# Product groups of 384 tokens that begin after three of batch 0's five query blocks

## The chip, the cores and the metric

One core of one Trainium2 chip runs the whole program. The metric is the device time in microseconds of one execution. TensorE (PE) multiplies and transposes, VectorE (DVE), ScalarE (ACT) and GpSimd (POOL) work on tiles, SyncE (SP) issues DMAs. ACT and POOL issue some DMAs too.

## The reference

Attention with a forgetting gate over 8 batches, 8 heads, 576 tokens and head width 64, then a two-layer product with a SiLU over all 4608 tokens.

```python
scores = scale * np.matmul(q, k.transpose(0, 1, 3, 2))
cum = np.cumsum(np.log(np.clip(f, 0.0001, 1.0)), axis=-1)
scores = np.where(causal, -1000000000.0, scores + cum[:, :, :, None] - cum[:, :, None, :])
attn = softmax(scores)                      # over the last axis
x = (attn @ v).transpose(0, 2, 1, 3).reshape(4608, 512)
h = x @ w_in                                # w_in 512 x 2048
out = (h * sigmoid(h)) @ w_out              # w_out 2048 x 512, out float32
```

All inputs are float32. The gate factors into a row factor, which the softmax cancels, and a column factor exp(-cum), which the kernel multiplies into v.

## The kernel before

The work on attention goes by **pairs** p of heads: four pairs in a batch, 32 in all. 576 tokens are five blocks, four of 128 and one of 64 (the tail).

For the first batches q and k come as float32 by SP (`load_main` into `whole`, `load_tail` into one of two `raw` tiles), POOL casts them (`cast_main`, `cast_tail`), TensorE transposes them (`turn_first`, `transposes`, result `tpqk`), and DVE copies them to qT and kT. Later batches come by casting DMAs on POOL's queue (`load_qk`, tiles `mp`) and DMA transposes on SP.

The decay is made once for all batches: `decay_clip`, `decay_sum`, `decay_turn`, result wT, the exps in L180 and L183. `prep_v(p)` on POOL multiplies v (vm) with wT into one of the `vaug` tiles, with wT itself as a 65th column.

`scores(p, t)` makes the transposed scores of pair p in four tiles t (TensorE L281, one exp each on ACT, L306, result uT). `attend_rows` multiplies with vaug (L349, `avr`), and DVE divides by the 65th column (L358, L359, result `xt`). `turn_pair` turns the rows to xT (TensorE `tpx` L371, ACT copy L377).

The product goes by **groups** g of TG = 512 tokens. `m1_chunk(g, fc)` is one of 16 chunks of the first layer: four matmuls (`hp`, L400), tanh on ACT (L411), one DVE operation (L412, result `gtile`). `m2_part(g, tb, part)` is a quarter of the second layer for 128 tokens: four matmuls (`po`, L425) with four of the 16 rows of w_out. After four parts ACT scales the result and SP writes it.

The order is written by hand: the program text under `manual_schedule` is the order on each engine, and each engine runs its list in order. So is each queue of DMA issues, SP's and POOL's. A DMA that must wait for a free tile holds up all issues behind it.

In front, batch 0 runs whole: all four pairs, all five blocks, then `m1_chunk(0, 0)` begins. Between the parts of batch 1 and later `work(n)` puts n chunks or parts, from two lists `m1_queue` and `m2_queue`; a group's second layer may begin when its first is through (`can_m2`). `pace(p)` says how many a pair gets; m1_ready says how many groups have their xT. Batch 1 can draw on group 0 alone.

The loads of the weights are on POOL's queue: w_in in two halves after the casts of pair 2, ahead of `prep_v(0)`; w_out in four quarters by rows (`load_rows`) behind these lines:

```python
cast_both(NPB)
cast_both(NPB + 1)
prep_v(NPB)
for c in range(0, NFC, NFC // 4):
    load_rows(w_out_bf, moe_w_out, c, c + NFC // 4)
```

`prep_v(NPB)` is that of pair 4, batch 1's first, and reads v of batch 1. The SP queue has batch 1's loads in the order tails, q and k (`load_main`), v.

Of the kernel before, what the change touches and what calls it, by code (L numbers as in the profile page):

```python
# [15 lines left out]
P = 128  # L16
# [3 lines left out]
def kernel(  # L20
# [38 lines left out]
    NVA = 3  # L59
# [4 lines left out]
    xp = ctx.enter_context(tc.tile_pool(name="xp", bufs=4))  # L64
# [4 lines left out]
    evp = ctx.enter_context(tc.tile_pool(name="evp", bufs=2))  # L69
    rp = ctx.enter_context(tc.tile_pool(name="rp", bufs=4))  # L70
    gpool = ctx.enter_context(tc.tile_pool(name="gpool", bufs=2))
# [6 lines left out]
    MOST = 9.0  # L78
    HOLD = 6
# [43 lines left out]
    def load_qk(b, c, which):  # L123
        t = sbp.tile([P, DM], BF16, name="mp", tag="mp", bufs=16)
        raw[b, c, which] = t
        nc.gpsimd.dma_start(  # L126
            out=t[: bs[c], :].rearrange("p (h d) -> p h d", h=H),
            in_=(q, k)[which][b, :, c * P : c * P + bs[c], :].rearrange("h p d -> p h d"),
        )
# [9 lines left out]
    f_sb = evp.tile([BH, S], FP32, name="f_sb", tag="ev")  # L139
# [14 lines left out]
    def decay_sum():  # L154
        lnf = f_sb
        cum = evp.tile([BH, S], FP32, name="cum", tag="ev")
        nc.vector.tensor_tensor_scan(
            out=cum[:, :], data0=lnf[:, :], data1=lnf[:, :], initial=0.0,
            op0=ALU.add, op1=ALU.bypass,
        )  # L160
        mid = const.tile([BH, 1], FP32, name="mid")
        nc.vector.tensor_scalar_mul(out=mid[:, :], in0=cum[:, S - 1 : S], scalar1=0.5)
        cumc = cum
        nc.vector.tensor_scalar(
            out=cumc[:, :], in0=cum[:, :], scalar1=mid[:, 0:1], scalar2=None,
            op0=ALU.subtract,
        )
        cums.append(cumc)
# [20 lines left out]
    def cast_main(b, j, which):  # L189
        m = sbp.tile([P, NB * 2 * D], BF16, name="m", tag="m", bufs=4)  # L190
        m = m.rearrange("p (c h d) -> p c h d", c=NB, h=2)
        cast[b, j, which] = m
        nc.gpsimd.tensor_copy(  # L193
            out=m[:, 0 : NB - 1, :, :].rearrange("p c h d -> p h c d"),
            in_=whole[b][:, which, 2 * j : 2 * j + 2, :].rearrange(
                "p h (c d) -> p h c d", c=NB - 1
            ),
        )

    def cast_tail(b, j, which):  # L200
        m = cast[b, j, which]
        nc.gpsimd.tensor_copy(
            out=m[:TAIL, NB - 1, :, :], in_=tails[b, which][:TAIL, 2 * j : 2 * j + 2, :]
        )

    def turn_first(which):
        qk_tiles(0) if 0 not in qkT else None
        m = cast[0, 0, which].rearrange("p c h d -> p c (h d)")
        tp = big([P, SM], BF16, "tpqk")
        for c in range(NB - 1):  # L210
            nc.tensor.transpose(tp[:, c * P : (c + 1) * P], m[:, c, :], ident_bf[:, :])
        nc.vector.tensor_copy(
            out=qkT[0][which][:, 0, 0:SM].rearrange("x (p c) -> x p c", c=NB - 1),
            in_=tp[:, :].rearrange("x (c p) -> x p c", c=NB - 1),
        )

    def turn_first_tails():
        tp = big([P, 2, TAIL], BF16, "tpqk")
        for which in range(2):
            m = cast[0, 0, which].rearrange("p c h d -> p c (h d)")  # L220
            nc.tensor.transpose(
                tp[:, which, :], m[:TAIL, NB - 1, :], ident_bf[:TAIL, :TAIL]
            )
        for which in range(2):
            nc.vector.tensor_copy(out=qkT[0][which][:, 0, SM:S], in_=tp[:, which, :])

    def transposes(p, which):
# [5 lines left out]
        for c in range(NB):  # L233
            n = bs[c]
            nc.tensor.transpose(  # L235
                tp[:, c * P : c * P + n], m[:n, c, :, :].rearrange("p h d -> p (h d)"),
                ident_bf[:n, :n],
            )
        dst = qkT[b][which][:, j, :]
# [6 lines left out]
    def prep_v(p):  # L246
# [3 lines left out]
        for c0, c1, n in ((0, NB - 1, P), (NB - 1, NB, TAIL)):  # L250
# [8 lines left out]
        nc.gpsimd.tensor_copy(  # L259
            out=va[:, :, :, D], in_=wT[:, :, 2 * j + b * H : 2 * j + 2 + b * H]  # L260
# [9 lines left out]
    def scores(p, t):  # L270
        qT, kT = (x[:, p % NPB, :] for x in qkT[p // NPB])
        u = us[p % 3]
        first = p < NPB
        sc = psc.tile([P, 2, 512], FP32, name="sc", tag="sc")
        adds = ([(0, P)], [(64, P)], [(0, P), (320, P)], [(0, TAIL)])[t]
        pe_adds = adds if first and t == 2 else []
        col = 0
        for kb, q0, n in TILES[t]:
            for i in range(2):
# [6 lines left out]
                    stop=not pe_adds,  # L286
                )
            for i in range(2) if pe_adds else ():
                nc.tensor.matmul(  # L289
                    sc[:, i, col : col + P],  # L290
                    lhsT=ident_bf[:, :],
                    rhs=maskadd[:, :],
                    start=False,
# [4 lines left out]
        if first and not pe_adds:  # L298
            for c0, nk in adds:
                nc.vector.tensor_tensor(  # L300
                    out=sc[:nk, :, c0 : c0 + nk],
                    in0=sc[:nk, :, c0 : c0 + nk],
                    in1=maskadd[:nk, None, 0:nk].to_broadcast([nk, 2, nk]),
                    op=ALU.add,
                )
# [3 lines left out]
        if first:  # L309
            return  # L310
# [11 lines left out]
    TG = 512  # L322
# [14 lines left out]
    def attend_rows(p, lohi=((0, 3), (3, NB))):  # L337
        b, j = divmod(p, NPB)
        u, va = us[p % 3], vaugs[p % NVA]
# [26 lines left out]
    def turn_pair(p):  # L366
        b, j = divmod(p, NPB)
        tp = big([P, S], BF16, "tpx")
        for c in range(NB):
# [6 lines left out]
        for x, at, o, n in x_parts(b * S, (b + 1) * S):  # L376
# [64 lines left out]
    m2_queue = [(g, tb, pt) for g in range(NG) for tb in range(4) for pt in range(4)]  # L441
# [17 lines left out]
    def can_m1():  # L459
# [3 lines left out]
        return g < m1_ready and (not m2_queue or m2_queue[0][0] > max(g - 2, min(g - 1, 0)))  # L463
# [4 lines left out]
    def work(n):  # L468
        nonlocal turn_m2
        for _ in range(n):  # L470
            if can_m2() and (turn_m2 or not can_m1()):
                m2_part(*m2_queue.pop(0))
                turn_m2 = False
            elif can_m1():
                m1_chunk(*m1_queue.pop(0))
                turn_m2 = True
            else:
                return
            spend(0.88)

    def have():
        return sum(1 for x in m1_queue + m2_queue if x[0] < m1_ready)

    def pace(p):
# [7 lines left out]
        for _ in range(20):  # L492
            k = NPB * (b + 1) - p + min(LAG, 3.5 * (b - 1)) / (2.3 + 0.88 * n)
# [58 lines left out]
    with tc.manual_schedule():  # L552
        nc.scalar.dma_start(out=f_sb[:, :], in_=f.rearrange("b h s -> (b h) s"))
        load_main(0, 0, 2)
        load_tail(0)
        load_main(0, 2, 4)
        for c in range(2):
            load_v(0, c, nc.sync)
        load_main(0, 4, H)
        for c in range(2, NB):  # L560
            load_v(0, c, nc.sync)

        def cast_both(p):
# [3 lines left out]
            for w in RAW[b]:  # L567
                cast_tail(b, j, w)
# [6 lines left out]
        for u in us:  # L575
            nc.vector.memset(u[:, :, uoff[4] + TAIL :], 0.0)
        for va in vaugs:
# [8 lines left out]
        for w in range(2):  # L586
            cast_main(0, 0, w)
        for w in range(2):
            cast_tail(0, 0, w)
        cast_both(1)  # L590
        cast_both(2)
        load_w(w_in_bf, moe_w_in, 0, DFF // 2)
        load_w(w_in_bf, moe_w_in, DFF // 2, DFF)
        for w in range(2):
            turn_first(w)
        scores(0, 0)
        turn_first_tails()
        scores(0, 1)
        decay_sum()
        scores(0, 3)  # L600
        transposes(1, 0)
        scores(0, 2)
        decay_turn()
        prep_v(0)
        transposes(1, 1)
        scores(1, 0)
        cast_both(3)
        load_tail(1)
# [4 lines left out]
        for p in range(1, NPB):  # L613
            more = p + 1 < NPB
            prep_v(p)
            scores(p, 1)
            if more:
                transposes(p + 1, 0)
            scores(p, 3)
            if more:  # L620
                transposes(p + 1, 1)
            if p > 1:
                turn_pair(p - 2)
            attend_rows(p - 1, LO)
            scores(p, 2)
            if more:
                scores(p + 1, 0)
            attend_rows(p - 1, HI)
        turn_pair(NPB - 2)
        attend_rows(NPB - 1, LO)  # L630
        attend_rows(NPB - 1, HI)
        m1_chunk(0, 0, begin=True)
        turn_pair(NPB - 1)
        m1_ready = 1
        cast_both(NPB)
        cast_both(NPB + 1)
# [3 lines left out]
        work(HOLD)  # L640
        transposes(NPB, 0)
        work(1)
        transposes(NPB, 1)
        work(2)
        due = 0.0
        for p in range(NPB, NP):
# [4 lines left out]
            due += pace(p)  # L651
            n = int(due)
            due -= n
            n1, n2 = (n + 2) // 3, (n + 1) // 3
            n3 = n - n1 - n2
# [15 lines left out]
            if p == NPB * NEARLY - 3:  # L671
                load_tail(NEARLY)
                load_main(NEARLY, 0, 4)
                load_main(NEARLY, 4, H)
            for fn in fetch.get(p, []):
                fn()
            if early:
                work(n2 // 2)
# [7 lines left out]
            work(n2 - n2 // 2 if early else n2)  # L686
# [6 lines left out]
            if j == NPB - 1:  # L693
                attend_rows(p)
                spend(1.2)
                if b < NTURN:
                    work(2)
# [4 lines left out]
        while m1_queue or m2_queue or later:  # L702
            n = len(m1_queue) + len(m2_queue)
            work(1)
# [30 lines left out]
```

## Time and profile before

| what | us |
|---|---|
| median of 3 runs | 359.93 (359.5 to 360.38) |
| profiled execution, its own time | 359.25 |
| its span, first to last instruction | 357.5 |
| first dense product (hp) on PE | 34.12 |
| first po on PE | 53.8 |
| end of the last matmul | about 354 |
| w_in issued / w_out issued on POOL | 14.39 / 41.33 |

The page gives busy time by engine and the span in 40 slices of 8.94 us; a digit is the busy share in tenths. A timeline line has start, length, engine, line of the code, operation, out<-in, count, and in brackets the idle time before it with what ended it. "to landing" is the time from the issue of a DMA to its completion.

### The profile page before, as it was taken

To read this page: it belongs to the slowest core of one execution; us is meant where nothing else is said; L and a number is where in the kernel's file an instruction comes from. 1 tells how busy PE (TensorE), PEld (TensorE's weight loads), DVE (VectorE), ACT (ScalarE), POOL (GpSimd) and SP (SyncE) were. 2 spreads that over 40 slices of the span, in tenths; PEclk is the share of its full clock that TensorE was granted. 3 is DMA by queue.
4 is the path that set the end of the run, shared out by engine and by line. 5 is a ranking of instruction groups with operands and counts; after the bars stand their busy time and mean duration, and the time that the engine had idled before them with its cause. 6 is when DMAs were issued, how large, how long until landed. Compare 5 with 4: busy or idle time off the path is not lost.

```text
span 357.5 us, 7026 instructions
## 1 busy us (share of the span) xinstructions
PE 336.3 (94%) x2656; PEld 168.4 (47%) x2697; DVE 191.7 (54%) x450; ACT 211.9 (59%) x345; POOL 119.6 (33%) x207
## 2 busy tenths in 40 slices
PE   2797989999999999999999999999999999999995
PEld 1455445554555445544454453444444454444442
DVE  4664895538743675348543791567237723744300
ACT  4566674558753986388647764676468615644421
POOL 5563598239554235423564250110301000000000
PEclk9999999999999999999999999999999999999999
DMA  8899999999997998399969994452240014000021
GB/s 220 213 208 315 192 193 222 155 210 170 148 150 117 163 150 78 89 170 142 124 122 152 130 166 123 100 117 75 74 83 31 1 68 118 2 29 29 31 76 71
DMA packets 142514, 44.92 MB, mean 126 GB/s; under 512 B 129616, under 2 KB 136784, under 8 KB 142480
## 3 DMA queue, kind: packets, MB, share of 16 engines
q1 hardware_dynamic: 87664, 33.64, 42.5%
q0 software_dynamic: 54736, 10.69, 38.4%
q8 instruction: 21, 0.34, 0.4%
q10 hardware_dynamic: 80, 0.15, 0.2%
q14 instruction: 13, 0.11, 0.1%
HBM read 36.85 MB, written 9.44 MB: 129 GB/s over the span
## 4 chain that ended last, share of the span: by engine, by line
PE 82%; DVE 6%; ACT 4%; DMA 3%; issue 3%; POOL 1%; SPq 0%; ACTq 0%
PE po L425 33%; PE hp L400 30%; PE avr L349 7%; PE sc L281 7%; DVE gtile L412 2%; ACT uT L306 2%; DMA xT<-xt 2%; PE tpx L371 2%; DVE uT L320 2%; PE tpqk L235 2%; ACT th L411 1%; DMA whole<-in_k_dram 1%; DVE xt L359 1%; PE sc L289 1%; DVE qT L240 1%
## 5 line engine op out<-in xcount | busy, mean ns | idle before, releaser
L400 PE MATMUL hp<-xT,w_in_bf 128*128 128x512 bf16 x556 | 135.8, 380 | 3.2 <-DVE gtile L412 0.8
L425 PE MATMUL po<-w_out_bf,gtile 128*128 128x512 bf16 x555 | 133.7, 379 | 1.4 <-DVE gtile L412 0.4
L412 DVE SCALAR_TENSOR_TENSOR gtile<-th,hp 128x512 bf16<-128x512 bf16 x144 | 96.0, 685 | 52.2 <-ACT th L411 50.3
L306 ACT ACTIVATE uT<-sc 128x1024 bf16<-128x1024 f32 (+1 forms) x128 | 101.3, 850 | 24.9 <-PE sc L281 15.9
L411 ACT ACTIVATE th<-hp 128x512 bf16<-128x512 f32 x144 | 84.8, 613 | 50.0 <-PE hp L400 46.2
L251 POOL TENSOR_TENSOR vaug<-vm,wT 128x512 bf16<-128x512 f32 x64 | 45.4, 729 | 132.7 <-PE avr L349 121.4
L400 PEld LDWEIGHTS <-w_in_bf 128*128 128x128 bf16 x576 | 53.1, 98 | 65.2 <-issue 6.1
L425 PEld LDWEIGHTS <-gtile 128*128 128x128 bf16 x576 | 53.6, 98 | 62.9 <-issue 2.4
L320 DVE TENSOR_TENSOR uT<-uT,mask 128x256 bf16<-128x256 bf16 (+1 forms) x112 | 35.3, 337 | 66.2 <-ACT uT L306 66.0
L434 ACT ACTIVATE osb<-po 128x512 f32<-128x512 f32 x36 | 21.7, 602 | 46.7 <-PE po L425 46.7
L281 PE MATMUL sc<-qT,kT 64*128 64x64 bf16 (+4 forms) x384 | 37.3, 287 | 5.5 <-ACT uT L306 2.2
L349 PEld LDWEIGHTS <-uT 128*128 128x128 bf16 x960 | 33.7, 98 | 6.4 <-issue 0.7
L349 PE MATMUL avr<-vaug,uT 128*128 128x65 bf16 x960 | 36.2, 195 | 0.2 <-POOL vaug L259 0.2
L359 DVE TENSOR_TENSOR xt<-avr,rr 128x384 bf16<-128x384 f32 x64 | 31.4, 491 | 2.3
L281 PEld LDWEIGHTS <-kT 64*128 64x128 bf16 x384 | 15.3, 95 | 30.1 <-issue 21.0
L126 POOL DMA_DIRECT2D mp<-in_k_dram x30 | 25.9, 865 | 1.0 <-DMA mp<-in_k_dram 1.0
L126 POOL DMA_DIRECT2D mp<-in_q_dram x25 | 22.2, 887 | 1.3 <-DMA w_out_bf<-in_moe_w_out_dram 0.5
L358 DVE RECIPROCAL rr<-avr 128x6 f32<-128x6 f32 x64 | 11.7, 183 | 18.6 <-PE avr L349 18.5
L377 ACT COPY xT<-tpx 128x512 bf16<-128x512 bf16 (+7 forms) x32 | 11.2, 404 | 17.0 <-PE tpx L371 16.9
L193 POOL CAST m<-whole 128x512 bf16<-128x512 f32 x20 | 11.9, 607 | 15.0 <-DMA whole<-in_q_dram 12.4
L235 PE MATMUL tpqk<-ident_bf,m 128*128 128x128 bf16 (+1 forms) x90 | 10.9, 241 | 0.3 <-DVE gtile L412 0.3
L235 PEld LDWEIGHTS <-m 128*128 128x128 bf16 (+1 forms) x90 | 7.3, 106 | 6.3 <-issue 1.6
(47 smaller groups left out, 71.8 us busy)
## 6 DMA issues: line engine op xcount, KB each, us to landing
out_dram<-osb SPq DMA_DIRECT2D x36, 256.0 KB, 2.2
vm<-in_v_dram SPq DMA_DIRECT2D x32, 256.0 KB, 4.7
mp<-in_k_dram POOLq DMA_DIRECT2D x24, 128.0 KB, 6.2
whole<-in_q_dram SPq DMA_DIRECT2D x5, 512.0 KB, 9.7
mp<-in_q_dram POOLq DMA_DIRECT2D x20, 128.0 KB, 4.8
w_in_bf<-in_moe_w_in_dram POOLq DMA_DIRECT2D x2, 1024.0 KB, 11.2
w_out_bf<-in_moe_w_out_dram POOLq DMA_DIRECT2D x4, 512.0 KB, 10.7
whole<-in_k_dram SPq DMA_DIRECT2D x3, 512.0 KB, 9.5
```

What stands on the lines that cost most here:

```text
L126: nc.gpsimd.dma_start(out=t[: bs[c], :].rearrange("p (h d) -> p h d", h=H), in_=(q, k)[which][b, :, c * P : c * P + bs[c], :].rearrange("h ...
L235: nc.tensor.transpose(tp[:, c * P : c * P + n], m[:n, c, :, :].rearrange("p h d -> p (h d)"), ident_bf[:n, :n],)
L251: nc.gpsimd.tensor_tensor(out=va[:n, c0:c1, :, 0:D], in0=vm[:n, c0:c1, 2 * j : 2 * j + 2, :], in1=wT[:n, c0:c1, 2 * j + b * H : 2 * j + 2 ...
L281: nc.tensor.matmul(sc[:, i, col : col + n], lhsT=kT[r, kb * P : (kb + 1) * P], rhs=qT[r, q0 : q0 + n], start=True, stop=not pe_adds,)
L306: nc.scalar.activation(out=u[:, :, o : o + col], in_=sc[:, :, 0:col], func=ACT.Exp, scale=scale)
L320: nc.vector.tensor_tensor(out=d, in0=d, in1=mk, op=ALU.mult)
L349: nc.tensor.matmul(av[:, qb - lo, i, :], lhsT=u[:, i, o : o + P], rhs=va[:, kb, i, :], start=(kb == 0), stop=(kb == qb),)
L359: nc.vector.tensor_tensor(out=xt[:, lo:hi, 2 * j : 2 * j + 2, :], in0=av[:, :, :, 0:D], in1=r[:, 0:n, :, None].to_broadcast([P, n, 2, D]), ...
L400: nc.tensor.matmul(hp[:, :], lhsT=w_in_bf[:, cc, fc * P : (fc + 1) * P], rhs=xg[g][:, cc, :], start=(cc == 0), stop=(cc == NCC - 1),)
L411: nc.scalar.activation(out=th[:, :], in_=hp[:, :], func=ACT.Tanh, scale=0.5)
L412: nc.vector.scalar_tensor_tensor(out=gte[:, fc, :], in0=th[:, :], scalar=1.0, in1=hp[:, :], op0=ALU.add, op1=ALU.mult,)
L425: nc.tensor.matmul(po[:, :], lhsT=gte[:, fc, tb * P : (tb + 1) * P], rhs=w_out_bf[:, fc, :], start=(fc == 0), stop=(fc == NFC - 1),)
```

## The change

- TG becomes 384, so a group has 16 first-layer chunks of 384 tokens and 3 times 4 parts. There are 12 groups in place of 9.
- Batch 0 is done in two portions: query blocks 0 to 2 of all four pairs (`scores_first(p, 0, t)`, `attend_first(p, 0)`, `turn_pair(p, 0, 3)`), then group 0's product begins, and blocks 3 and 4 follow between its chunks. The causal mask of batch 0 is added by TensorE alone.
- `prep_v` is split for batch 0: blocks 0 to 2 (VLO) early, 3 and 4 (VHI) later. There are four vaug tiles.
- w_in comes in four column parts, the first behind `prep_v(0, VLO)`. The tails of q and k are cast for all heads at once (`cast_tails`). SP loads q and k of batch 0 by two heads; its tails move behind them.
- `spin(n)` runs matmuls over a zeroed row of w_out's tile on TensorE, 13 in all.
- `work` counts microseconds (0.66 a chunk, 0.87 a part) in place of pieces. Buffers: gtile 3, xT 5, mp 14. f and its sums live in a tile of `xt`.

The diff, cut:

```diff
-    NVA = 3
+    idle = w_out_bf[:, 0, :]
+    NVA = 4
...
-    xp = ctx.enter_context(tc.tile_pool(name="xp", bufs=4))
+    xp = ctx.enter_context(tc.tile_pool(name="xp", bufs=5))
-    gpool = ctx.enter_context(tc.tile_pool(name="gpool", bufs=2))
+    gpool = ctx.enter_context(tc.tile_pool(name="gpool", bufs=3))
-    MOST = 9.0
-    HOLD = 6
+    MOST = 8.0
+    HP, PO = 0.66, 0.87
...
+    def cast_tails(b):
+        for which in RAW[b]:
+            t = sbp.tile([P, DM], BF16, name="tc", tag="tc", bufs=4)
+            cast[b, which] = t
+            nc.gpsimd.tensor_copy(
+                out=t[:TAIL, :].rearrange("s (h d) -> s h d", h=H),
+                in_=tails[b, which][:TAIL, :, :],
+            )
...
+    def spin(n):
+        ps = big([P, SM], FP32, "spin")
+        for _ in range(n):
+            nc.tensor.matmul(
+                ps[:, :], lhsT=idle[:, 0:P], rhs=idle[:, :], start=True, stop=True
+            )
...
-    TG = 512
+    TG = 384
+    NTB = TG // P
...
-        return g < m1_ready and (not m2_queue or m2_queue[0][0] > max(g - 2, min(g - 1, 0)))
+        return g < m1_ready and (not m2_queue or m2_queue[0][0] > (0 if g == 2 else g - 3))
...
     with tc.manual_schedule():
+        nc.vector.memset(idle[:, :], 0.0)
         nc.scalar.dma_start(out=f_sb[:, :], in_=f.rearrange("b h s -> (b h) s"))
         load_main(0, 0, 2)
-        load_tail(0)
-        load_main(0, 2, 4)
-        for c in range(2):
-            load_v(0, c, nc.sync)
-        load_main(0, 4, H)
-        for c in range(2, NB):
-            load_v(0, c, nc.sync)
+        load_main(0, 2, 4)
+        load_v(0, 0, nc.sync)
+        load_v(0, 1, nc.sync)
+        load_main(0, 4, 6)
+        load_v(0, 2, nc.sync)
+        load_main(0, 6, H)
+        load_tail(0)
+        load_v(0, 3, nc.sync)
+        load_v(0, 4, nc.sync)
...
+        VLO, VHI = ((0, 3, P),), ((3, 4, P), (4, NB, TAIL))
+        cast_both(0)
+        cast_both(1)
+        spin(7)
+        turn_main(0, 0)
+        spin(4)
+        rest = turn_main(0, 1, P // 4)
+        decay_sum()
+        rest()
+        spin(2)
+        scores_first(0, 0, 0)
+        turn_main(1, 0)
+        turn_main(1, 1)
+        scores_first(0, 0, 1)
+        decay_turn()
+        scores_first(1, 0, 0)
+        cast_both(2)
+        prep_v(0, VLO)
+        load_in(0)
+        cast_both(3)
+        prep_v(1, VLO)
+        load_in(1)
+        prep_v(2, VLO)
+        prep_v(3, VLO)
+        cast_tails(0)
+        load_in(2)
+        load_in(3)
         load_tail(1)
         load_main(1, 0, 4)
         load_main(1, 4, H)
         for c in range(NB):
             load_v(1, c, nc.sync)
...
+        attend_first(3, 0)
         m1_chunk(0, 0, begin=True)
+        m1_chunk(0, 1, begin=True)
+        turn_pair(3, 0, 3)
         m1_ready = 1
+        turn_tails()
+        work(HP)
+        scores_first(0, 1, 0)
+        work(HP)
+        scores_first(0, 1, 1)
+        for p in range(NPB):
+            prep_v(p, VHI)
+            if p == 1:
+                cast_both(NPB)
+            if p == 2:
+                cast_tails(1)
+                cast_both(NPB + 1)
+            work(HP)
+            if p + 1 < NPB:
+                scores_first(p + 1, 1, 0)
+            work(HP)
+            attend_first(p, 1)
+            if p + 1 < NPB:
+                scores_first(p + 1, 1, 1)
+            work(HP)
+            turn_pair(p, 3, NB)
         prep_v(NPB)
         for c in range(0, NFC, NFC // 4):
             load_rows(w_out_bf, moe_w_out, c, c + NFC // 4)
-        work(HOLD)
         transposes(NPB, 0)
-        work(1)
+        work(HP)
         transposes(NPB, 1)
-        work(2)
```

## The prediction

> **What bounds the kernel now.** I read the page first: engine totals and the 40 slices.
>
> ```profile
> span 357.5 us, 7026 instructions
> ...
> PE 336.3 (94%) x2656; PEld 168.4 (47%) x2697; DVE 191.7 (54%) x450; ACT 211.9 (59%) x345; POOL 119.6 (33%) x207
> ...
> PE   2797989999999999999999999999999999999995
> ```
>
> TensorE is the bound from the fifth slice on. Only the front, up to the first dense product at 34.12 us, has real holes, and that is what the change rebuilds. So I ask what limits the front, and what it hands over to. Next the timeline of TensorE, early and later.
>
> ```profile
> 4.51 0.61 PE L211 MATMUL tpqk<-ident_bf,m 128*128 128x128 bf16 x4 [4.51 <-POOL m L193]
> ...
> 34.12 4.69 PE L400 MATMUL hp<-xT,w_in_bf 128*128 128x512 bf16 x21 [0.67 <-ACT xT L377]
> 38.65 0.52 PE L235 MATMUL tpqk<-ident_bf,m 128*128 128x128 bf16 x5
> ```
>
> Four transposes took 0.61 us at the start, five took 0.52 us later: until about 23.4 us the array ran near half speed, although the granted clock reads 1.00 throughout. Now the timeline of POOL, which issues the weight loads.
>
> ```profile
> 39.85 1.40 POOL L251 TENSOR_TENSOR vaug<-vm,wT 128x512 bf16<-128x512 f32 x2 [4.49 <-DMA vm<-in_v_dram]
> 41.20 0.22 POOL L259 CAST vaug<-wT 128x10 bf16<-128x10 f32 x1
> 41.33 3.03 POOL L542 DMA_DIRECT2D w_out_bf<-in_moe_w_out_dram  x4
> ...
> 57.33 0.88 POOL L126 DMA_DIRECT2D mp<-in_q_dram  x1 [0.52 <-DMA w_out_bf<-in_moe_w_out_dram]
> ```
>
> The w_out loads stand behind `prep_v(4)`, which waited for v of batch 1 until 39.85. The view of w_out_bf gives their landing, and TensorE's timeline their first use:
>
> ```profile
> L425 PE MATMUL po<-w_out_bf,gtile x555: 376/379/390, 53.8 to 353.2; 128*128 128x512 bf16 x185
> DMA to landing us min/median/max: 8.1/10.7/13.5
> ```
>
> ```profile
> 53.79 1.02 PE L425 MATMUL po<-w_out_bf,gtile 128*128 128x512 bf16 x3 [0.37 <-DVE gtile L412]
> 54.75 0.42 PE L281 MATMUL sc<-qT,kT 64*128 64x320 bf16 x6
> ...
> 56.12 2.76 PE L425 MATMUL po<-w_out_bf,gtile 128*128 128x512 bf16 x12
> 58.71 0.52 PE L371 MATMUL tpx<-ident_bf,xt 128*128 128x128 bf16 x5
> ```
>
> The first quarter landed at 41.3 + 8.1 = 49.4, the last at 43.6 + 13.5 = 57.1; TensorE's fourth po part, which needs that last quarter, began about 57.8 and ended at 58.7. Under 1 us of slack: w_out is already just in time. A quicker front gains only if w_out comes earlier too.
>
> **Does w_out come earlier?** In the changed program POOL's order is still `prep_v(4)`, then the four w_out loads; `prep_v(4)` still waits for v of batch 1; on SP that stands behind q and k of batch 1 and its tails, which wait for POOL's `cast_tails(0)`, because there are two raw tiles. SP's timeline of before:
>
> ```profile
> 19.00 0.59 SPq L110 DMA_DIRECT2D raw<-in_q_dram  x1
> ...
> 29.16 11.78 SPq L118 DMA_DIRECT2D vm<-in_v_dram  x8
> ```
>
> So I walk POOL. The decay weights wT were ready at 13.57. Now: k's cast ends 5.9 as before, transposes 0.6, quarter copy 0.3, scan with its two followers 2.0, rest of the copy 0.55, scores 0.5, turn of the sums 0.4, the exponential ahead 0.8, two exps 0.6: 11.65. Then on POOL: three-block multiply 0.84 (on the line from 407 ns at 128 columns to 1052 at 512) and weight copy 0.23; w_in part 0.8; two casts 1.2; multiply and copy 1.07; w_in part 0.8; two more preps 2.1; two tail casts 1.2 (row: 607 ns at 128x512). End at 19.9, against SP's 19.00 before: batch 1's loads start about 0.9 us later, not earlier.
>
> What they then meet: w_in's parts 3 and 4, issued 19.9 to 21.5. Such a load starts to move about 2 us after its issue (w_in: 14.39 to 16.3) and the software queue moves 0.2 MB a microsecond (0.93 MB from 45 to 50 us). 1.05 MB with its slow first microseconds end near 28.5; in the run before w_in ended at 28, and the SP queue, starved by it (0.02 MB a us from 23 to 27), moved batch 1's 3.5 MB in the 12.5 us from 27.3 to 39.85. Now it can use gaps between 21 and 23: v of batch 1 at 39.5. Bounds: 37.6 (16.6 us of transfers from 21, nothing lost), 41.5 (all the starving of before, and POOL a microsecond later). `prep_v(4)` 1.5: w_out is issued at 41.0, its first quarter there at 49.1, its last 41.0 + 15.8 = 56.8.
>
> The Trainium skill speaks for less: its page DMA: Bandwidth & Descriptors, section Anatomy of one DMA — SWDGE (gpsimd) path, fits 2.0 us plus bytes over 436e3, an estimate of 11.6 us for w_out's 4.19 MB; by that the sum below would be 4.2 us less. The trace's 15.8 us disagrees, and I go by the trace.
>
> **When does TensorE ask for it?** The three-block phase ends when `prep_v(3)` does, about 18.7; first hp near 20, when the first w_in quarter lands (12.7 + 8.1 = 20.8 at most). Then 16 hp chunks of 0.65 between the rest of batch 0. `cast_both(4)` on POOL stands ahead of `prep_v(2, VHI)` and `prep_v(3, VHI)` and waits for batch 1's k (32.7 before), so the last row blocks of pair 3 start near 37.4; from there avr 0.55, three hp chunks 1.95, four sets of transposes 1.6 and scores 0.56 bring TensorE to its first po part near 42.5. It waits there until 49.1, with batch 1's attention queued behind; then for each quarter until 56.8, and ends the fourth po part at 57.7. In the run before that point was 58.7.
>
> **What is left behind that point.** Before: 128 hp chunks of 0.864 = 110.6. After: 176 of 384 tokens; from 216 ns at 512 columns and 30 ns at 65 (0.91 us for 30 avr), 163 ns at 384, chunk 0.651: 114.6. That is +4.0, of which 3.5 is simply 128 tokens fewer in group 0, the only product work there is before w_out. TensorE's order has also not yet done what before had done by its 58.7: pair 4's 30 avr 0.91, second half of scores 5 0.35, two sets of transposes for pair 6 0.90: +2.2. po parts left are 140 in both. Everything later is the same work on a full TensorE (idle between 60 and 340 us: 4.4 us), so nothing is won back.
>
> Hidden, with their cover: 13 spin matmuls and the doubled speed in front (cover: the 6.6 us wait for w_out; without the wait they would count, the spins up to 5.6 us at half speed, the speed some 7 us the other way); 48 more gtile operations (551 ns each by the 1.05 ns a column of L359: +7 us) and tanh (508 ns: +9 us) on engines busy 54 and 59%, bounds 0 to +2 us on TensorE; two more SP issues, tails moved behind q, k and v of block 2, needed only near 21; the further buffers 0.
>
> Sum against the profiled run's 359.25: + (57.7 - 58.7) + 6.2 = 364.4. The median, 359.93, is 0.7 above that run: 365.
>
> **Rivals.** *TensorE is never kept waiting* (faster). v and w_out land early enough for the first po part at 42.5; then the fourth ends at 42.5 + 3.5 + 1.4 = 47.4, and the sum is 354.2, as a median 355. For it: DMA had holes from 15 to 16 and at 43 us. Against it: the loads' order, and 4.19 MB that took 15.8 us. It breaks even where the last quarter lands at 51.6, which needs w_out issued by 35.8, before v of batch 1 can be there at its best bound (37.6).
>
> *The long wait cools the array* (slower still). The trace shows half speed from 4.5 until 23.4, ended only inside the first stretch without a gap (from 17.7). If a 6.6 us hole brings it back, the last po part takes 0.9 longer and up to 4 us of dense work behind it lose 2: 368. The trace has no such hole later, so neither for nor against. The Trainium skill, TensorE: Matmul & The Clock Gate, Part 1, says that one idle window of some 3.4 us halves the clock and a busy one restores it; by that this would happen.
>
> *The spins don't do what they say*: the front stays at half speed and po is asked for near 48. The sum stays 365, as that is still before 49.1.
>
> **How the numbers follow.** Forecast with w_out deciding: 365, chance 0.63 (with the spin rival in it). Cooling: 368, 0.19. Never waiting: 355, 0.12. Transfers at their best bounds, near 359 to 361: 0.06. The range: v at 37.6 and w_out in 14.2 us (2 to start, 10.5 at 0.2 MB a us, 1.7 to land) give 361.7; v at 41.5 gives 367, with cooling 370. 360.5 to 369.5 leaves out the rival on the other side and little else. A measurement of this kernel tells about 0.2% from no change: faster 0.14, same 0.03, slower 0.83.
>
> **What would show it.** The profile after: w_out issued near 41 and landing to 57; TensorE idle some 6 us before the first po, released by the DMA of w_out_bf; 384-column matmuls 163 ns apart; batch 1's SP loads at 20. I am wrong if the first po starts before 46, or if v of batch 1 is there before 36.

## The result, and the profile after

The changed kernel took 370.23 us as a median (369.27 to 372.58, four runs) against 359.73 us (359.5 to 360.38). The ratio is 1.0298, 95% interval 1.0248 to 1.0349: slower, as forecast, but by 10.5 us where 5 were forecast, and just above the range. The profiled execution took 372.58 us, the longest of the four; the others, of which there is no trace, lie 2.1 to 3.3 us lower. One execution each of a_tails_late, c_both, j_main_only and n_lag below ran in the chip's slower state; their ratios leave it out, their medians do not.

The page, in the rows shown of before, and the row of the granted clock:

```profile
span 370.8 us, 7637 instructions
...
PE 346.0 (93%) x2907; PEld 190.2 (51%) x2942; DVE 199.0 (54%) x489; ACT 218.4 (59%) x393; POOL 121.0 (33%) x198
...
PE   6989858886999999999999899999999999999995
...
PEclk9559999998999999999999999999999999999999
```

A slice is now 9.27 us. Three things are to be seen. The first two slices are busier than before. The sixth, at 46 to 56 us, is down to 5. And the tenth, at 83 to 93 us, is down to 6, where before had a 9; the clock row dips there too. TensorE's timeline in the front:

```profile
23.37 2.11 PE L470 MATMUL hp<-xT,w_in_bf 128*128 128x384 bf16 x6
...
49.22 1.02 PE L495 MATMUL po<-w_out_bf,gtile 128*128 128x512 bf16 x3
...
52.61 1.02 PE L495 MATMUL po<-w_out_bf,gtile 128*128 128x512 bf16 x4 [1.55 <-DMA w_out_bf<-in_moe_w_out_dram]
...
55.20 1.02 PE L495 MATMUL po<-w_out_bf,gtile 128*128 128x512 bf16 x4 [1.02 <-DMA w_out_bf<-in_moe_w_out_dram]
57.70 1.02 PE L495 MATMUL po<-w_out_bf,gtile 128*128 128x512 bf16 x4 [1.49 <-DMA w_out_bf<-in_moe_w_out_dram]
58.56 0.39 PE L253 MATMUL tpqk<-ident_bf,m 128*128 128x128 bf16 x4
```

The product begins 8.7 us earlier: its first hp is at 23.37, and before ran the first two at 32.04, the rest from 34.12. But the fourth po part ends at 58.56 against 58.71: TensorE waits 4.1 us for w_out in three pieces. POOL's timeline, and then the view of w_out_bf, say when that was issued and landed. (The row names PE for the wait ahead of `prep_v(4)`; in the trace the fourth 128-token block of batch 1's v landed at 41.29 and the tail's at 42.39, and the last quarter of w_out at 57.66.)

```profile
41.96 1.40 POOL L273 TENSOR_TENSOR vaug<-vm,wT 128x512 bf16<-128x512 f32 x2 [4.57 <-PE hp L470]
43.31 0.22 POOL L282 CAST vaug<-wT 128x10 bf16<-128x10 f32 x1
43.44 3.03 POOL L625 DMA_DIRECT2D w_out_bf<-in_moe_w_out_dram  x4
```

```profile
DMA to landing us min/median/max: 5.7/9.3/12.0
```

SP's timeline, batch 1's loads:

```profile
19.40 0.59 SPq L110 DMA_DIRECT2D raw<-in_q_dram  x1
...
28.01 12.14 SPq L118 DMA_DIRECT2D vm<-in_v_dram  x7
```

Up to here before and after stand level at 58.6 us. What follows does not. TensorE around the tenth slice:

```profile
83.17 2.77 PE L470 MATMUL hp<-xT,w_in_bf 128*128 128x384 bf16 x16
88.91 4.44 PE L470 MATMUL hp<-xT,w_in_bf 128*128 128x384 bf16 x16 [2.97 <-DVE gtile L482]
```

The same 16 matmuls take 2.77 us ahead of the gap and 4.44 behind it. The windows around it, cut where the granted clock changes, have busy times and then PEclk:

```profile
core 0: us, PE busy (x) PEld busy (x) DVE busy (x) ACT busy (x) POOL busy (x), PEclk, DMA share, GB/s
...
11.00:28.10 17.10, 15.69 (x137) 9.32 (x135) 6.73 (x15) 7.77 (x15) 11.34 (x21) 0.50 1.25 205
28.10:89.50 61.40, 48.58 (x514) 28.18 (x515) 36.05 (x86) 37.09 (x66) 36.85 (x60) 1.00 1.39 195
89.50:92.90 3.40, 3.40 (x13) 1.62 (x11) 1.86 (x4) 1.47 (x3) 3.40 (x5) 0.50 1.57 186
```

What DVE and POOL did while TensorE waited:

```profile
84.43 3.96 DVE L387 TENSOR_TENSOR uT<-uT,mask 128x512 bf16<-128x512 bf16 x2
88.32 2.60 DVE L482 SCALAR_TENSOR_TENSOR gtile<-th,hp 128x384 bf16<-128x384 bf16 x5
```

```profile
84.93 1.45 POOL L273 TENSOR_TENSOR vaug<-vm,wT 128x512 bf16<-128x512 f32 x2
86.28 0.25 POOL L282 CAST vaug<-wT 128x10 bf16<-128x10 f32 x1
86.42 0.89 POOL L195 CAST m<-whole 128x512 bf16<-128x512 f32 x1
87.27 1.40 POOL L273 TENSOR_TENSOR vaug<-vm,wT 128x512 bf16<-128x512 f32 x2
```

Two mask multiplications of pair 8 (2.41 and 1.63 us in the trace) hold DVE for 3.96 us while POOL works without a pause. Their usual lengths are 0.43 and 0.21 us (medians). The groups by form give the means over the whole run, 0.51 and 0.27 us, with the long ones in them.

```profile
L387 DVE TENSOR_TENSOR uT<-uT,mask 128x512 bf16<-128x512 bf16 x28 | 14.2, 508 | 11.4 <-ACT uT L375 10.9
...
L387 DVE TENSOR_TENSOR uT<-uT,mask 64x128 bf16<-64x128 bf16 x28 | 7.7, 274 | 0.0
```

Behind the masks in DVE's order stand the gtile operations, which free the four PSUM tiles that hp takes in turn with the other large products. Four chunks of 0.65 us are 2.6 us of work, and a DVE that is away for 4 us stops TensorE. Before had a like burst on POOL (82.62 to 87.4), and the same two masks took 0.63 and 1.09 us. There four chunks are 3.5 us of work, and TensorE stood for 0.44 us. DVE's and TensorE's timelines of before:

```profile
83.38 1.65 DVE L320 TENSOR_TENSOR uT<-uT,mask 128x512 bf16<-128x512 bf16 x2
```

```profile
81.62 3.61 PE L400 MATMUL hp<-xT,w_in_bf 128*128 128x512 bf16 x16
85.68 1.02 PE L400 MATMUL hp<-xT,w_in_bf 128*128 128x512 bf16 x4 [0.44 <-DVE gtile L412]
```

**A ledger.** For each kernel I counted the matmuls still to run at some instants, at their pitch in the traces (hp 163 ns at 384 columns and 216 at 512, po 216, avr 30, a score 76, a transpose 88). The time to the last matmul less that work is what TensorE loses, idle or slow. All in us, from the profiled executions; the last three columns are experiments below.

| | before | after | h_pe_mask8 | m_turn5 | o_turn5_quarter |
|---|---|---|---|---|---|
| work left at 58.6 | 289.3 | 295.5 | 297.0 | 298.1 | 294.1 |
| lost 58.6 to 97 | 1.6 | 9.3 | 4.1 | 3.8 | 3.2 |
| lost 97 to 200 | 2.9 | 0.2 | 0.6 | 0.1 | 0.3 |
| lost 200 to 215 | 0 | 1.7 | 3.6 | 0 | 0.8 |
| lost after 215 | 1.1 | 1.4 | 1.7 | 1.7 | 0.9 |
| last matmul ends | 353.5 | 366.7 | 365.6 | 362.3 | 357.9 |

After minus before at the end is 13.1, where the forecast had 5.2: 6.2 of work left, 7.7 lost between 58.6 and 97, 1.7 between 200 and 215 and 0.3 later, less 2.7 that before loses between 97 and 200 and after does not; the rest is rounding. The losses are what the work leaves over, so an error of the pitches goes into them, about the same in every column.

### The profile page after: what moved, and what is told of

It is laid out like the page before. It is cut to its first block, busy times and chain, and to the rows that moved or that the text cites. A ratio compares the mean times of both kernels' runs of the same rounds, so it can differ in the third digit from the quotient of the medians.

```text
span 370.8 us, 7637 instructions
## 1 busy us (share of the span) xinstructions
PE 346.0 (93%) x2907; PEld 190.2 (51%) x2942; DVE 199.0 (54%) x489; ACT 218.4 (59%) x393; POOL 121.0 (33%) x198
## 4 chain that ended last, share of the span: by engine, by line
PE 77%; DMA 6%; ACT 5%; DVE 5%; issue 3%; SPq 2%; POOL 1%; ACTq 0%; POOLq 0%; DVEq 0%
PE po L495 30%; PE hp L470 30%; PE avr L417 7%; PE sc L366 5%; DMA w_out_bf<-in_moe_w_out_dram 3%; ACT uT L375 2%; PE tpx L439 2%; DVE gtile L482 2%; ACT th L481 1%; DVE uT L387 1%; DMA xT<-xt 1%; SPq L100 1%; DMA whole<-in_k_dram 1%; POOL mp L126 1%; DVE xt L344 1%
## 5 line engine op out<-in xcount | busy, mean ns | idle before, releaser
L470 PE MATMUL hp<-xT,w_in_bf 128*128 128x384 bf16 x768 | 148.2, 332 | 4.1 <-DVE gtile L482 3.0
L482 DVE SCALAR_TENSOR_TENSOR gtile<-th,hp 128x384 bf16<-128x384 bf16 x192 | 102.8, 552 | 66.3 <-ACT th L481 61.0
L481 ACT ACTIVATE th<-hp 128x384 bf16<-128x384 f32 x192 | 92.0, 503 | 66.6 <-PE hp L470 61.4
L470 PEld LDWEIGHTS <-w_in_bf 128*128 128x128 bf16 x768 | 71.8, 99 | 60.8 <-issue 8.7
L375 ACT ACTIVATE uT<-sc 128x1024 bf16<-128x1024 f32 x112 | 88.3, 849 | 19.3 <-PE sc L366 19.3
L273 POOL TENSOR_TENSOR vaug<-vm,wT 128x512 bf16<-128x512 f32 (+2 forms) x68 | 46.6, 710 | 118.1 <-DMA vm<-in_v_dram 60.3
L366 PE MATMUL sc<-qT,kT 64*128 64x512 bf16 (+1 forms) x336 | 29.4, 277 | 1.8 <-DVE kT L262 1.4
L427 DVE TENSOR_TENSOR xt<-avr,rr 128x384 bf16<-128x384 f32 (+1 forms) x56 | 27.5, 491 | 2.0
L447 ACT COPY xT<-tpx 128x384 bf16<-128x384 bf16 (+1 forms) x32 | 11.6, 401 | 14.8 <-PE tpx L439 14.8
L318 ACT ACTIVATE uT<-sc 128x768 bf16<-128x768 f32 (+1 forms) x16 | 13.4, 839 | 8.3 <-PE sc L310 8.2
```

What stands on the lines that cost most here:

```text
L273: nc.gpsimd.tensor_tensor(out=va[:n, c0:c1, :, 0:D], in0=vm[:n, c0:c1, 2 * j : 2 * j + 2, :], in1=wT[:n, c0:c1, 2 * j + b * H : 2 * j + 2 ...
L366: nc.tensor.matmul(sc[:, i, col : col + n], lhsT=kT[r, kb * P : (kb + 1) * P], rhs=qT[r, q0 : q0 + n], start=True, stop=True,)
L375: nc.scalar.activation(out=u[:, :, o : o + col], in_=sc[:, :, 0:col], func=ACT.Exp, scale=scale)
L427: nc.vector.tensor_tensor(out=xt[:, lo:hi, 2 * j : 2 * j + 2, :], in0=av[:, :, :, 0:D], in1=r[:, 0:n, :, None].to_broadcast([P, n, 2, D]), ...
L470: nc.tensor.matmul(hp[:, :], lhsT=w_in_bf[:, cc, fc * P : (fc + 1) * P], rhs=xg[g][:, cc, :], start=(cc == 0), stop=(cc == NCC - 1),)
L481: nc.scalar.activation(out=th[:, :], in_=hp[:, :], func=ACT.Tanh, scale=0.5)
```

## The experiments

Ratios are to the kernel before on the same chip, with 95% intervals.

**The group size alone.** The kernel before with smaller groups:

```diff
-    TG = 512
+    TG = 384
+    NTB = TG // P
...
-    m2_queue = [(g, tb, pt) for g in range(NG) for tb in range(4) for pt in range(4)]
+    m2_queue = [(g, tb, pt) for g in range(NG) for tb in range(NTB) for pt in range(4)]
```

> The kernel before with groups of 384 tokens and nothing else of the change (12 groups, three token blocks in a group, its own pacing of 0.88 a piece). Theory of the sum: the front has 3.5 us less product before w_out is there, the fourth po part still ends near 58, so 128 tokens more are left: +3 to +4 us, 363 to 364, with waits for w_out_bf in the profile that before had not. Rival (w_out's landing is not what counts; a smaller group merely starts po earlier): within 1 us of 360.

365.11 us, 1.0123 [1.0081, 1.0165]: 3 to 6 us of the 10.5 come with the group size, without any of the new front. That is near the 3 to 4 us of the theory, but only in part by its mechanism. In the trace the fourth part ends at 58.2, with 0.69 us of waiting for w_out, and counted as in the ledger the work left at 58.6 is 2.7 us more than before; but 6.5 us are lost from 58.6 to 97. There is a gap of another kind, released by POOL's cast of q and k, and the clock was halved from 80.3 to 83.7:

```profile
78.77 0.53 PE L235 MATMUL tpqk<-ident_bf,m 128*128 128x128 bf16 x5 [2.19 <-POOL m L193]
```

**The spins left out.** The lines `spin(7)`, `spin(4)`, `spin(2)` taken out:

> The 13 spin matmuls are left out; their results are not used. Prediction's view: what the front gains is hidden by the wait for w_out, so the front runs at half speed to about 28 us and the fourth po part still ends near 58.6: 370, within 1 us. Rival (the front's speed counts, since wT and with it the w_in loads come later): w_out issued 1 to 2 us later and 371.5 or more.

371.14 us, 1.0304 [1.0259, 1.0349]: they are worth nothing that can be measured. Without them half speed lasted until 16.8 us (four transposes took 0.61 us at 4.19) and came back from 44.1 to 47.5; with them the array was fast from 4.2 to 11.0 and then half until 28.1.

**w_out issued earlier**, ahead of `prep_v(4)`:

```diff
-        prep_v(NPB)
         for c in range(0, NFC, NFC // 4):
             load_rows(w_out_bf, moe_w_out, c, c + NFC // 4)
+        prep_v(NPB)
```

> The four w_out loads go ahead of prep_v(4) on POOL's queue, so they no longer wait for v of batch 1; all else as in the changed kernel. Theory that w_out's landing sets the front: issued near 37.5 instead of 43.4, last quarter there near 53.5, fourth po part ends near 54.5 instead of 58.6, about 4 us gained: 366. Rival (the sum of all transfers sets the front: v of batch 1 comes as much later as w_out comes earlier, and pair 4's attention waits for it): within 1 us of 370.

371.56 us, 1.0307 [1.0236, 1.0379]: no gain. POOL's timeline and TensorE's last wait:

```profile
37.56 3.03 POOL L625 DMA_DIRECT2D w_out_bf<-in_moe_w_out_dram  x4
```

```profile
55.92 1.41 PE L495 MATMUL po<-w_out_bf,gtile 128*128 128x512 bf16 x4 [2.37 <-DMA w_out_bf<-in_moe_w_out_dram]
```

Issued 5.9 us earlier, the fourth part starts only 1.8 us earlier: the last quarter took up to 16.1 us to land instead of 12.0, beside batch 1's loads, and the last block of batch 1's v landed at 45.95 instead of 42.39, as the rival has it. Half speed from 56.4 to 59.8 took some of the gain too (the four matmuls took 1.41 us, not 1.02).

**Batch 1's q and k ahead of its tails** on SP:

```diff
-        load_tail(1)
         load_main(1, 0, 4)
         load_main(1, 4, H)
+        load_tail(1)
```

> The changed kernel, with q and k of batch 1 ahead of batch 1's tails on SP, so that they don't wait for the two raw tiles. Transfers theory: the queues idle about half the time from 15 to 22 us; these 2.1 MB fill it, v of batch 1 is there about 4 us earlier, w_out issued near 39.5 instead of 43.4, the fourth po part ends near 55: 366 to 367. Rival (the end of batch 1 near 78 us is pinned by something else than w_out, since with w_out issued 6 us earlier it was 78.0 too): fourth po part earlier, batch 1's end within 1 us of 78, 370.

372.28 us, 1.0307 [1.0256, 1.0358]. w_out was issued at 43.90, not earlier, and group 1's first layer began at 79.0 (in the changed kernel at 78.76).

**POOL's long wait taken away.** In the changed kernel `cast_tails(2)` stands at pair 5 and holds POOL for 9.59 us (until 63.33) for a tile from SP. Moved to pair 6, behind the loads of q and k:

```diff
                 load_main(NEARLY, 4, H)
-                cast_tails(NEARLY)
             for fn in fetch.get(p, []):
                 fn()
+            if p == NPB * NEARLY - 2:
+                cast_tails(NEARLY)
```

> The cast of batch 2's tails moves on POOL's queue from pair 5 to pair 6, behind the mp loads; nothing else changes. Queue theory: in the changed kernel POOL stood from 53.8 to 63.3 us behind this cast, its work was pushed into 80 to 90 us, there a DVE mask pair took 3.96 us instead of about 0.8, TensorE got a hole of 2.97 us and ran at half speed behind it. Without the block: mp loads issued from about 54, mask pair under 1.2 us, no hole over 1 us, clock 0.98 or more; 365 us (363.5 to 367), the time that the sum of the prediction gives. Rival (the 5 us above the prediction come from the smaller groups or from a clock that falls anyway): 369 to 371.

370.54 us, 1.0267 [1.0194, 1.0341]: no gain that can be told from the noise. Its trace is of its longest execution (375.23 us). The gap stays: 2.45 us before 89.22, behind masks of 1.89 and 1.63 us. POOL's pile-up is not a matter of that one wait.

**Both**, w_out first and tails late:

> Both edits of the two kernels before. If the two waits are in series, the gains add: about 9 us, 361 (359 to 363). If POOL's block by the tails is only a consequence of the late w_out (the first output, which holds up SP, waits for it), the gain is that of the larger one alone: 365 to 366.

370.43 us, 1.0268 [1.0205, 1.033]: neither gain shows. In the trace, again of the longest execution (375.22 us), the gap is 3.25 us, again behind the masks (one took 3.9 us), and half speed follows from 87.6 to 91.0.

**Pair 8's mask by TensorE.** The mask is added to the scores by two matmuls a diagonal block, as in batch 0, and DVE's two operations on uT go, for that pair alone:

```diff
+    PEM = (8,)
...
+            for i in range(2) if diag else ():
+                w = min(n, P)
+                nc.tensor.matmul(
+                    sc[:, i, col : col + w],
+                    lhsT=ident_bf[:, :],
+                    rhs=maskadd[:, 0:w],
+                    start=False,
                     stop=True,
                 )
...
+        if on_pe:
+            return
         if t == 2:
```

> The changed kernel, with the causal mask of pair 8 alone (batch 2's first) added by TensorE in PSUM instead of multiplied by DVE over two tiles of SBUF; ten short matmuls more, 0.6 us. Port theory: the hole of TensorE at 82 to 89 us comes from DVE's masks, which read two SBUF tiles while POOL works (2.41 and 1.63 us instead of 0.33 and 0.43). Without them the gtile operations of pair 8 run at once, no hole over 1 us between 79 and 93, no fall of the clock there: 3 to 5 us less than 370.2, 366. Rival (POOL's or ACT's own lateness makes the hole): a hole of 2 us or more stays, 370.

371.48 us, 1.0301 [1.0255, 1.0347]. TensorE's timeline and DVE's in that place:

```profile
84.52 5.36 PE L484 MATMUL hp<-xT,w_in_bf 128*128 128x384 bf16 x32
```

```profile
84.63 0.18 DVE L267 COPY qT<-tpqk 128x64 bf16<-128x64 bf16 x1
86.03 4.97 DVE L496 SCALAR_TENSOR_TENSOR gtile<-th,hp 128x384 bf16<-128x384 bf16 x8 [1.22 <-ACT th L495]
```

32 matmuls at 168 ns without a gap: so the gap and the half speed hung on the mask operations. POOL still ran its whole burst (86.17 to 91 us). The other runs say the same by size. In the eight traces of the new kernel in which DVE multiplies this mask (after, a_tails_late, b_wout_first, c_both, d_no_spin, j_main_only, k_quarter, n_lag; some follow below) the two operations took 1.82 to 4.44 us, and TensorE's gap behind them, 0.83 to 3.32 us, was shorter by 1.0 to 1.1 us in every one. In the five with this mask on TensorE (h_pe_mask8, i_all, l_lag, m_turn5, o_turn5_quarter) there is no gap over 0.15 us in that place. The loss from 58.6 to 97 falls from 9.3 to 4.1 us, yet the span is only 1.1 us shorter, and the median not at all. TensorE's timeline and SP's further on say why:

```profile
207.69 0.61 PE L369 MATMUL sc<-qT,kT 64*128 64x512 bf16 x6
211.75 0.82 PE L484 MATMUL hp<-xT,w_in_bf 128*128 128x384 bf16 x4 [3.46 <-DMA xT<-xt]
```

```profile
207.71 1.71 SPq L522 DMA_DIRECT2D out_dram<-osb  x1
209.48 1.64 SPq L466 DMA_TRANSPOSE xT<-xt  x1
```

The last block of batch 4, the first batch turned by DMA transposes, stands on SP behind a store of a result, and TensorE, which keeps to its order, waits for it. The changed kernel waits 1.06 us there, this one 3.46. The rest of the gain went into 1.5 us more work left at 58.6: 0.8 for the mask itself, and 0.7 in a front where the wait for w_out was 5.0 us in place of 4.1.

**All four edits** (w_out first, q and k first, tails late, pair 8's mask):

> All edits so far on the changed kernel: w_out ahead of prep_v(4), q and k of batch 1 ahead of the tails, batch 2's tails cast at pair 6, pair 8's mask on TensorE. If the two causes (late w_out, the hole at 82 to 89) are what the prediction's sum lacked and more, the gains add: 358 to 361, level with before. If batch 1's end is pinned otherwise: 365 to 367.

370.53 us, 1.0284 [1.0255, 1.0313]: the gap is gone here as well (4.2 us lost from 58.6 to 97), and 4.3 us are lost from 200 to 215 instead.

**One quarter of w_out:**

```diff
-                rhs=w_out_bf[:, fc, :],
+                rhs=w_out_bf[:, fc % (NFC // 4), :],
...
-        for c in range(0, NFC, NFC // 4):
-            load_rows(w_out_bf, moe_w_out, c, c + NFC // 4)
+        load_rows(w_out_bf, moe_w_out, 0, NFC // 4)
```

> Only the first quarter of w_out is loaded (one load, 1.05 MB instead of 4.19 MB), and every quarter of the second layer multiplies by those rows: three quarters of w_out are left out of the result. Theory (w_out's landing sets where TensorE stands until 58.6 us): the waits for w_out of 4.1 us in the changed kernel shrink to at most 1.5 us (the first quarter), the fourth second-layer part ends near 55 instead of 58.6, and the time falls by 2.5 to 4 us, to 366 to 368. Rival (the front hands over to v of batch 1 and to the casts, w_out is only what is waited for last): the fourth part ends earlier but the end of batch 1's scores and attention stays at 78 to 80 us, the gap of 3 us with its half speed behind it stays, and the time falls by less than 1.5 us.

368.62 us, 1.0232 [1.0195, 1.0269]. TensorE waited 2.4 us for the quarter that is left, and the fourth part ended at about 56.5. The gain of 1.6 us lies between theory and rival and is not clear of the noise, as the interval overlaps with that of the changed kernel; in the traces the fourth part ends 2 us earlier. So w_out's landing costs about 2 us at most. Group 1's first layer began at 76.5, 2 us earlier, and the loss behind it remains (8.7 us from 58.6 to 97).

**The product further behind attention**, on top of pair 8's mask, and alone (`LAG = 10.0` becomes 16.0):

> The run with pair 8's mask on TensorE, and in addition the product is allowed to trail further behind attention (LAG 16 instead of 10), so that TensorE has other work when batch 4's turned rows come late. Theory (closing the gap at 82 to 92 us only brought TensorE earlier to the DMA-turned rows of batch 4, where it waited 3.5 us): TensorE's wait for xT near 210 us falls below 1 us, its idle and slow time between 200 and 215 us from 3.6 to about 1.5 us, and the time falls by 2 to 3 us against that run, to about 368. Rival (the loss is not in that wait): no change within 1 us, because the work held back comes at the end without attention beside it.

> The changed kernel with LAG 16 instead of 10 and nothing else. Theory (its own wait for xT is 1.1 us, the 5 us that the forecast lacked lie between 78 and 97 us): the loss between 78 and 97 us stays at 5 to 6 us, the time falls by 0 to 1 us. Rival (the pacing of the product is what costs, wherever it shows): the time falls by 2 us or more.

370.74 us, 1.0293 [1.0254, 1.0331], and 375.03 us, 1.0382 [1.0327, 1.0438]. Neither theory holds; the first run is what its rival gave. The waits for xT were 3.1 us in both (the longest 2.71): hardly less than 3.46 in the first, and three times the 1.06 of the changed kernel in the second, where a gap of 3.26 us was also followed by half speed from 88.9 to 95.7. More lag is no cover for this wait. And the second has the gap and the long wait together, so the wait is not only what a closed gap leaves.

**Batch 4 turned by TensorE**, on top of pair 8's mask (`NTURN = 4` becomes 5):

> The run with pair 8's mask on TensorE, and in addition batch 4 is turned by TensorE (NTURN 5 instead of 4) rather than by the DMA. Theory (the waiting time that the closed gap at 82 to 92 us gave free came back as the wait for batch 4's turned rows): the 3.5 us wait for xT near 210 us is gone, TensorE has four more sets of transposes (4 x 0.45 = 1.8 us), idle and slow time from 200 to 215 us falls from 3.6 to about 1 us, the span falls by 1 to 2 us against that run, to about 368. Rival (the wait for xT returns at batch 5): the loss moves to 235 to 250 us, and the time stays.

367.83 us (367.26 to 368.87), 1.0236 [1.0209, 1.0263]. Nothing is lost from 200 to 215 us, the wait does not come back at batch 5 (0.8 us lost from 230 to 250), and the span is 3.5 us shorter than with the mask alone. So the wait for batch 4's rows had taken what the closed gap gave free; with both gone, the kernel is 2.4 us below the changed kernel by the medians, though the two ratios' intervals still overlap at their ends. No run turned batch 4 by TensorE and left the mask to DVE, so what the turn alone is worth is not shown.

**All three together**, mask, turn and one quarter of w_out:

> All three at once: pair 8's mask on TensorE, batch 4 turned by TensorE, and one quarter of w_out in place of four (three quarters of w_out are left out of the result). Theory (the surplus over the forecast is the sum of the gap with half speed at 82 to 97 us, the waits for w_out, and the waits of TensorE that follow): the idle and slow time between 58.6 and 97 us is below 3 us (9.3 in the changed kernel), between 200 and 215 us below 1.5 us, the span is 362 to 365 us, and what stays above the kernel before is the work of the smaller groups and what the edits add (0.8 and 1.8 us on TensorE). Rival (the slow front is what TensorE pays, in whichever gap): other waits take their place between 60 and 97 us, and the span stays above 367 us.

364.99 us (363.71 to 367.13), 1.0158 [1.0126, 1.019]. Its page:

```profile
span 361.9 us, 7724 instructions
...
PE   7888769999999999999999999999999999999995
```

The tenth slice is a 9 again. The span is a hair below the bounds given, the loss from 58.6 to 97 a little above its bound (3.2 us), from 200 to 215 within (0.8). In the ledger its last matmul ends 4.4 us behind that of before: it has 4.8 more work left at 58.6, and its losses later are 0.4 smaller. None of the 13 kernels is as fast as the kernel before.

## Why the prediction was wrong in size

**The anchor: right, in part by luck.** It put w_out's issue at 41.0, the last quarter at 56.8 and the end of the fourth part at 57.7; they came at 43.44, about 57.7 and 58.56. Two errors cancelled: the issue was 2.4 us late, as batch 1's v was (41.29 against 39.5), and from first issue to last landing went 14.2 us, not 15.8. TensorE reached its first po only at 49.2, not 42.5: the first hp was at 23.37 (forecast: near 20), and half speed held until 28.1. So it waited 4.1 us in three pieces rather than 6.6 at once, and the end stayed where w_out put it. Where the front ran at full speed, as in m_turn5, the forecast's course shows: first hp at 20.5, po asked for at 44.9, a wait of 4.53 us to 49.4. That w_out decides is right too, but for some 2 us at most: k_quarter got back 1.6, which is within the noise, and an earlier issue (b_wout_first) nothing.

**The +6.2 behind it: right.** The ledger has 295.5 against 289.3 at 58.6 us. The pitch of 163 ns held (16 matmuls in 2.77 us: the 15 pitches between them and one of 0.33). The group size alone cost 5 us (e_before_384) where the forecast's share for it was 4.0; that they are so near is luck, as in its trace only 2.7 us are work left and the rest is lost between 58.6 and 97.

**"Everything later is the same work on a full TensorE, so nothing is won back": this is the step that failed.** Nothing was won back, but 9.3 us were lost between 58.6 and 97 where before loses 1.6. About 5 of them are the gap of 2.97 us and the half speed behind it (4.44 instead of 2.77 us for 16 matmuls, so 4.6 together): h_pe_mask8 and m_turn5 lose 4.1 and 3.8 there. The rest, some 2 to 3 us more than before, is smaller waits on DVE and POOL, which no run took apart.

**Within it, the bound of 0 to +2 us** for more gtile operations on engines that are busy 54 and 59% was the mis-sized term: where it was to be paid, TensorE lost 4.6 us. It took the cover from the share over the whole span. What counts is how long DVE is away at one place, 3.96 us here. That the groups are smaller explains only a part: the masks' 1.65 us before and the 1.82 to 4.44 us after gave gaps shorter by 1.2 and by 1.0 to 1.1 us, so most of the gap comes from longer masks, and the forecast has no term for these.

That the long masks come from POOL working at the same time is not shown by a run, as none took POOL's work away there; but in the traces the two go together. Of the 1660 mask operations in the 15 traces, 1154 ran while POOL neither computed nor issued a DMA, and none of them took over 1.02 times its usual length (0.43, 0.29 and 0.21 us for the three shapes). All 163 that took over 1.2 times as long ran beside work of POOL: 138 beside operations that compute, 25 beside DMA issues alone. The Trainium skill's page SBUF — State Buffer, section SBUF: two separate sides, says that VectorE with two SBUF inputs and a GpSimd operation that reads SBUF exclude each other for a whole instruction. The trace fits that rule: the masks, which read uT and the mask from SBUF, took 2.41 and 1.63 us with POOL's operations beside them, and POOL's cast 0.89 us instead of 0.60. Why the same two masks took 1.82 us in b_wout_first and 4.44 in k_quarter stays open.

**The rival of the cooling array** had the right mechanism; in the changed kernel it came at another place. The waits for w_out were too short for it there (no half speed from 28.1 to 89.5), the gap at 86 to 89 was not. Its price is 1.7 us. Where TensorE stood longer for w_out, 3.6 to 5.3 us in h_pe_mask8, l_lag, m_turn5 and n_lag, half speed did come at the place forecast, and was over by 53.9 to 56.3 us, ahead of the fourth part. The rival with no waiting (355) did not come near. That the spins are worth nothing was right (d_no_spin).

**What stays open.** The three traceless runs of the changed kernel are 2.1 to 3.3 us shorter than the traced one, so the median holds less loss than the ledger; which part is missing there can't be told. Nor is it shown how the 5 us by which the medians miss the forecast divide: m_turn5 got back 2.4 of them and o_turn5_quarter, which leaves out three quarters of w_out, 5.2, with edits that cost work of their own.

## What to carry to other kernels

Moving work to an earlier place pays only as far as the next thing in line allows: name the load that is asked for next, and price what has not been done by then. When a tile of the main loop shrinks, count the cover that the buffers give in microseconds (buffers times the shorter chunk, less what is already used up) against the longest time for which the engine that frees them can be away at one place, not against its mean share: here operations of 0.2 and 0.4 us took 4 us together in one place. And when a gap is closed and the time does not move, look for the next wait in order of time: here it was 120 us later, and with that one gone too the median fell.

## What the runs showed of the hardware

A wait need not be long for half speed to follow: it did behind gaps of 2.97 us (after), 3.25 (c_both) and 2.19 (e_before_384), not behind 2.45 (a_tails_late) or 1.66 (d_no_spin); with the 3.62 us for w_out in h_pe_mask8 it came from 49.5 to 56.3. Nor does a busy row keep it up: TensorE was busy for 15.69 of the 17.10 us that the changed kernel spent at 0.50 from 11.0 to 28.1, with small transposes, scores and rows. The same front was halved for one window in l_lag and not at all from 6.1 to 47.1 in m_turn5, as the windows of those two runs show:

```profile
10.70:14.20 3.50, 3.38 (x34) 2.12 (x32) 1.56 (x3) 2.09 (x5) 2.85 (x5) 0.51 1.24 256
```

```profile
6.10:47.10 41.00, 31.79 (x374) 19.13 (x373) 24.34 (x53) 26.08 (x45) 22.97 (x42) 1.00 1.13 225
```

The columns are as in the windows above, PEclk ahead of the DMA share: 0.51 in the first, 1.00 in the second. So where in such a front the clock is halved is not fixed by the code of the front.
